# Sums of a Strassen-Winograd product on GpSimd, more W_in runs by seven products, and a new order

## The chip, the cores and the metric

The kernel runs on one core of a Trainium2 chip. A core has five engines with queues of their own: TensorE (PE, matmuls; its weight loads are shown as PEld), VectorE (DVE), ScalarE (ACT), GpSimd (POOL) and SyncE (SP, which here issues DMAs alone). Each engine takes its instructions in order; semaphores make one engine wait for another. The metric is the device time of one execution in microseconds (us), the median of several runs.

## The reference

Attention over a window of 96 positions and 8 global ones, with a bias that falls with the distance, then two matrices with a function between:

```python
# q, k, v: (4, 8, 768, 64); w_in: (512, 2048); w_out: (2048, 512); scale = 1/8
scores = scale * q @ k^T - slope[h] * dist      # kept where 0 <= i - j < 96 or j < 8
a = softmax(scores); attn = a @ v               # (4, 8, 768, 64)
x = attn.transpose(0, 2, 1, 3).reshape(3072, 512)
h = x @ w_in
g = h - tanh(h)
out = g @ w_out                                 # (3072, 512), float32
```

## The kernel before

The 3072 rows are 24 units of 128 rows. A unit's queries and keys come in by DMA (`lq`, `lk`, with values `lv`), are transposed (`T`, on TensorE for the first seven units and by a transposing DMA on SP for the rest), multiplied (`S`), put through the exponential (`E`, ScalarE), masked (`M`, VectorE, line 405, from the fourth unit on), multiplied with the values (`AV`), scaled by the inverse of the row sum (`R`, `N`) and transposed again (`X`, `Xe`). `K` and `V` are small copies of the global keys and values.

Units are then grouped for the first matrix: two groups of one unit, five of two, three of four (groups 7, 8 and 9). For a column block f of 128 of the 2048 columns, `m1` is a product of W_in with the group's transposed rows (line 470), `th` its tanh (ScalarE, line 567) and `g` the difference (VectorE, line 581), written as bfloat16 into `gall`. With four units a block is four matmuls of 128x512.

The table DUNITS names runs of four column blocks (group, run) that are computed in another way: as a 2x2 by 2x2 block product with seven instead of eight half-size products (the Strassen-Winograd scheme). `v1` to `v4` are its sums of W_in (VectorE, line 502), once for each run number, `y1` to `y4` its sums of the group's rows (line 507), `d1` to `d7` the seven products of four 128x256 matmuls each (line 529), `e0` to `e2` copies of partial results from PSUM (ScalarE, line 272), `q11`, `q21`, `q22` three adds (VectorE, lines 540 and 543). Tanh and difference then stand at lines 554 and 560. Before, runs 2 and 3 of groups 8 and 9 are done so.

The second matrix is done in the same scheme for each pair of units (a, a+1), twelve pairs: `w1` to `w4` are sums of W_out, computed once (line 608). `n1` to `n4` are sums of blocks of `gall` (`g_sum`, line 610; 128x1024 bfloat16 each, two of them in place): `n1` is read by `n2` and by product `p5`, `n2` by `n4` and `p6`, `n3` by `p7`, `n4` by `p3`. The products `p1` to `p7` are eight matmuls of 128x256 (line 636). `a0` to `a2` copy partial results, `c11` to `c22` add up the output blocks (line 650), `st` stores a unit's rows. For the last pair (22), `p3` and `c12` are split into two halves.

No scheduler orders this. The string ORDER lists each step's word, with a suffix for its engine where the step may go to more than one (`/a` ScalarE, `/d` VectorE, `/p` GpSimd, `/s` SyncE); the program issues the words in that order, and each engine's queue is the list filtered to it. The string HOMES gives the buffer or PSUM bank of each tile. GpSimd issues nearly all loads and some of the stores; an instruction that waits on GpSimd's queue holds back the loads behind it. A load there waits until the eighth load before it has landed.

Of the kernel before, what the change touches and what calls it, by code (L numbers as in the profile page):

```python
# [27 lines left out]
Xe.5/d th.0.12 g.2.14 m1.3.6 E.6.1 g.0.12 m1.3.8 n3.0 th.3.6 lk.10 E.6.0 n2.0 m1.3.4 g.3.6 K.6/a m1.3.2 n1.2 w1.0
m1.3.12 th.3.2 lk.8 g.0.8 th.3.8 p1.0 w1.1 m1.3.10 w3.0 a0.0/a th.3.12 g.3.2 m1.3.0 lv.6 th.3.10 w2.0 p2.0 w2.1 lq.10
w3.1 p6.0 T.7 lv.7 w4.1 p7.0 g.3.8 a1.0/a V.5/a n2.2 p5.0 th.3.0 T.9 n3.2 g.3.12 p1.2 a2.0/a w4.0 p2.2 a0.2/a g.3.10  # L30
th.3.4 p6.2 c11.0 T.8 c22.0 M.6.0 p4.0 a1.2/a n4.2 p5.2 g.3.0 g.3.4 p7.2 a2.2/a c21.0 c11.2 p3.2 st.1.0/p T.10 v1.3
M.6.1 lk.12 S.7 c12.2/a c22.2 lk.14 AV.6 n4.0 E.7.1 p4.2 V.6/d lk.11 R.6 E.7.0 N.6/d m1.3.14 lk.13 M.7.1 X.6 M.7.0
th.3.14 p3.0 lq.12 Xe.6/a c21.2 g.3.14 AV.7 lq.11 c12.0/a K.7/d R.7 S.8 N.7/d lv.8 n1.4 X.7 lv.9 E.8.1 p1.4 Xe.7/d n2.4
lv.10 m1.4.8 E.8.0 v1.2 v2.3 lq.13 m1.4.10 a0.4/a M.8.1 th.4.8 K.9/a p6.4 g.4.8 th.4.10 E.9.0 g.4.10 m1.4.14 a1.4/d S.9
V.7/d th.4.14 M.9.0 T.11 g.4.14 p5.4 E.9.1 M.8.0 T.12 m1.4.4 E.10.0 n3.4 p2.4 M.9.1 st.3.0/s th.4.4 M.10.0 E.10.1 AV.8
n4.4 m1.4.0 T.13 lq.15 K.10/a R.8 a2.4/a N.8/d AV.9 th.4.0 g.4.4 p3.4 Xe.8 R.9 N.9/d m1.4.2 c12.4/a c11.4 Xe.9 m1.4.6
g.4.0 st.4.0/p th.4.2 M.10.1 lq.14 m1.4.12 th.4.6 g.4.2 lv.11 p7.4 g.4.6 th.4.12 lk.15 S.10 c22.4 V.9/d lv.13 g.4.12
p4.4 E.11.0 n1.6 st.2.0/p p2.6 E.12.0 K.11/d lv.12 n3.6 AV.10 n2.6 K.12/a E.11.1 lk.16 p1.6 R.10 c21.4 lq.16 N.10/a
m1.5.10 a0.6/d M.11.1 p6.6 c11.6 th.5.10 S.11 T.15 a1.6/d g.5.10 p5.6 E.13.1 M.12.0 T.14 m1.5.8 V.10/d n4.6 E.13.0
M.11.0 m1.5.14 Xe.10 E.12.1 M.13.1 AV.11 th.5.14 p7.6 R.11 th.5.8 a2.6/d M.12.1 N.11/a m1.5.12 V.11/d v3.2 p3.6 g.5.14  # L40
th.5.12 M.13.0 Xe.11 m1.5.0 c12.6/a c22.6 st.6.0/p g.5.8 m1.5.2 th.5.0 lv.14 T.16 g.5.12 AV.12 g.5.0 th.5.2 lq.19 m1.5.6
R.12 N.12/d lk.18 m1.5.4 th.5.6 g.5.2 lq.18 p4.6 g.5.6 th.5.4 lq.17 g.5.4 S.12 V.12/d lv.16 c21.6 p1.8 n1.8 E.14.1 lv.15
m1.6.4 a0.8/d E.14.0 K.15/d v2.2 lk.17 AV.13 n2.8 th.6.4 m1.6.14 K.14/d lk.19 R.13 E.15.0 g.6.4 p6.8 N.13/d th.6.14 T.18
p2.8 g.6.14 a1.8/a M.14.0 Xe.12 S.13 n4.8 p5.8 c11.8 E.16.1 st.5.0/s v4.3 M.14.1 m1.6.10 E.16.0 M.15.0 T.17 AV.14 n3.8
E.15.1 m1.6.12 R.14 N.14/d T.19 th.6.10 m1.6.0 M.15.1 m1.6.2 a2.8/d th.6.0 Xe.14 M.16.0 V.14/a m1.6.6 g.6.0 th.6.2 Xe.13
g.6.10 AV.15 th.6.6 m1.6.8 g.6.2 g.6.6 p3.8 th.6.8 R.15 N.15/d th.6.12 p7.8 c12.8/a g.6.8 Xe.15 K.16/a st.8.0/p p1.10
g.6.12 lv.19 c22.8 S.14 n1.10 a0.10/a lq.21 n2.10 p4.8 E.17.1 lv.17 M.16.1 p6.10 E.17.0 V.15/d lk.20 p2.10 a1.10/d lk.23
v4.2 c21.8 p5.10 K.17/d lk.21 n4.10 st.9.0/s AV.16 M.17.1 a2.10/a lv.18 E.18.0 m1.7.15 R.16 N.16/d lq.22 p3.10 th.7.15
c11.10 lq.20 g.7.15 S.15 V.16/d c12.10/d lk.22 m1.7.6 M.17.0 E.19.0 lq.23 m1.7.7 E.19.1 M.19.0 lv.20 m1.7.5 M.18.0
th.7.6 T.21 th.7.7 m1.7.10 g.7.6 th.7.5 n3.10 m1.7.11 E.18.1 M.19.1 AV.17 th.7.10 g.7.5 m1.7.12 th.7.11 M.18.1 T.20  # L50
m1.7.2 R.17 g.7.7 th.7.12 N.17/d m1.7.9 Xe.16 th.7.2 g.7.12 AV.19 g.7.2 th.7.9 m1.7.0 T.22 V.17/d R.19 g.7.11 m1.7.4
th.7.0 g.7.9 st.7.0/s K.19/a m1.7.3 T.23 N.19/d th.7.4 v3.3 m1.7.8 g.7.10 Xe.17 g.7.0 p7.10 th.7.8 V.19/d th.7.3 g.7.8
m1.7.1 st.10.0/s Xe.19 g.7.4 m1.7.14 th.7.1 g.7.3 m1.7.13 c22.10 th.7.14 g.7.1 p4.10 g.7.14 th.7.13 g.7.13 S.16 c21.10
p1.12 n1.12 E.21.0 n2.12 p2.12 E.20.1 n3.12 AV.18 a0.12/d K.21/a E.20.0 p6.12 R.18 N.18/d K.20/a n4.12 S.17 Xe.18
a1.12/a c11.12 M.21.0 p5.12 E.22.1 M.20.1 p7.12 a2.12/d E.21.1 n1.14 p3.12 K.22/a M.20.0 E.22.0 S.18 c22.12 n2.14
c12.12/a p4.12 E.23.1 st.12.0/p n3.14 lv.23 m1.8.1 c21.12 E.23.0 y1.8 lv.21 d1.8.2 y2.8 p2.14 M.22.1 e0.8.2/a lv.22
M.21.1 th.8.1 d6.8.2 M.23.0 AV.20 p1.14 R.20 V.20/d M.22.0 d2.8.2 a0.14/a n4.14 m1.8.2 e1.8.2/a y3.8 N.20/a c11.14 p6.14
M.23.1 g.8.1 d7.8.2 th.8.2 d5.8.2 a1.14/d AV.21 q11.8.2 e2.8.2/a p5.14 R.21 V.21/a N.21/d d3.8.2 g.8.2 Xe.21 AV.22
th.8.9 q22.8.2 m1.8.0 th.8.8 R.22 y4.8 V.22/a Xe.20 m1.8.4 N.22/d g.8.9 d4.8.2 th.8.4 st.0.0/s d1.8.3 g.8.8 th.8.0 Xe.22
d2.8.3 q21.8.2 e0.8.3/a AV.23 g.8.4 th.8.11 d6.8.3 m1.8.5 R.23 q11.8.3 e1.8.3/a N.23/d d5.8.3 d7.8.3 g.8.0 Xe.23  # L60
e2.8.3/a m1.8.7 th.8.5 q22.8.3 th.8.10 d3.8.3 g.8.11 a2.14/a d4.8.3 th.8.7 g.8.5 m1.8.3 th.8.12 q21.8.3 p3.14 g.8.7
th.8.15 g.8.12 m1.8.6 th.8.13 g.8.15 d2.9.2 th.8.6 g.8.13 m1.9.2 c12.14/a y1.9 th.8.14 st.14.0/s g.8.6 m1.9.0 th.9.2
st.13.0/s y2.9 th.8.3 g.8.14 d1.9.3 d1.9.2 g.8.3 p7.14 e0.9.2/a g.8.10 e0.9.3/a m1.9.1 n1.16 th.9.0 y3.9 d6.9.2 c22.14
th.9.1 d6.9.3 g.9.2 p4.14 e1.9.3/a g.9.0 e1.9.2/a g.9.1 d5.9.3 d2.9.3 y4.9 e2.9.3/a d7.9.3 n2.16 d5.9.2 q22.9.3 p1.16
e2.9.2/a q11.9.2 d4.9.3 c21.14 a0.16/d d7.9.2 st.15.0/p m1.9.4 q22.9.2 st.11.0/p n3.16 d3.9.3 th.9.4 d3.9.2 q11.9.3
p6.16 th.9.9 q21.9.3 th.9.13 g.9.9 d4.9.2 a1.16/a m1.9.6 th.9.8 g.9.4 n1.18 p5.16 th.9.6 q21.9.2 th.9.12 m1.9.3 g.9.6
g.9.12 p1.18 th.9.14 g.9.13 a2.16/a th.9.15 p2.16 n3.18 a0.18/a th.9.3 p7.16 c11.16 n2.18 m1.9.7 c22.16 g.9.8 p2.18
g.9.15 th.9.11 p4.16 th.9.10 g.9.11 g.9.3 m1.9.5 n4.18 p6.18 n4.16 p7.18 g.9.14 a1.18/a th.9.5 g.9.10 p5.18 th.9.7 g.9.5
p3.16 a2.18/d c21.16 p2.20 g.9.7 st.17.0/s c12.16/a st.16.0/s n1.20 p1.20 n2.20 p3.18 a0.20/a c22.18 c11.18 p6.20 n3.20
c12.18/a st.18.0/s p4.18 a1.20/d n1.22 p5.20 n3.22 p7.20 n2.22 a2.20/a c21.18 p1.22 c22.20 st.19.0/s c11.20 p2.22  # L70
a0.22/a p6.22 c11.22 n4.22 st.22.0/s p4.20 a1.22/a p5.22 c21.20 n4.20 st.21.0/p p7.22 a2.22/a p3.20 c22.22 p4.22
# [758 lines left out]
```

## Time and profile before

| what | value |
|---|---|
| median of 3 runs | 202.23 us (202.12 to 202.49) |
| the profiled execution's own time | 202.65 us |
| its span, first to last instruction | 200.9 us |
| TensorE clock granted | 1.0 throughout |
| VectorE sums of `g_sum` | 48 of 128x1024, 684 ns each |
| GpSimd busy | 72.9 us, nearly all of it DMA issues of 0.6 to 0.9 us |

The profile is of one execution. Busy time of an engine is shown as a sum, a share of the span, or by groups of instructions of one source line; a group's row has its count, its busy time and the mean of one, then the idle time of the engine just before these instructions and what ended it. The chain of waits follows the work that ended last back to the start. A busy share of 97% says that an engine is a candidate, and the stretches of time say where.

### The profile page before, as it was taken

Reading aid. Unit: us, or ns where it says so; the run is one execution under the profiler, and the core shown is the slowest. Engines: PE = TensorE matmul, PEld = TensorE weight load, DVE = VectorE, ACT = ScalarE, POOL = GpSimd, SP = SyncE. Lnnn points to the kernel's source line nnn. Section 1 sums busy time; section 2 is a strip of 40 time slices with the busy share of each in tenths; the row PEclk is TensorE's granted clock in tenths of the full one; section 3 lists DMA queues with packets and bytes.
Section 4 is the critical chain, followed back from the end, with each engine's and each line's share of the span. In section 5 each row is a group of like instructions: output and inputs, shape, how many; then the busy total and the mean of one; then the engine's idle time right before and its main releaser. Section 6 shows DMA issues by size and latency. Waiting matters only on the chain.

```text
span 200.9 us, 5510 instructions
## 1 busy us (share of the span) xinstructions
PE 194.4 (97%) x2195; PEld 155.5 (77%) x2195; DVE 178.5 (89%) x375; ACT 132.6 (66%) x245; POOL 72.9 (36%) x93
## 2 busy tenths in 40 slices
...
GB/s 145 217 184 184 195 166 207 198 156 145 144 194 161 192 160 182 131 169 152 207 155 145 167 156 167 210 28 58 74 51 110 66 43 104 0 3 106 90 96 131
DMA packets 103755, 27.36 MB, mean 136 GB/s; under 512 B 93921, under 2 KB 101345, under 8 KB 103729
## 3 DMA queue, kind: packets, MB, share of 16 engines
...
q14 instruction: 10, 0.07, 0.1%
HBM read 27.26 MB, written 6.29 MB: 167 GB/s over the span
## 4 chain that ended last, share of the span: by engine, by line
PE 69%; DMA 13%; DVE 8%; POOL 7%; issue 1%; ACT 0%; POOLq 0%; DVEq 0%
PE ps L636 31%; PE ps L470 24%; DMA w_out_bf<-in_moe_w_out_dram 7%; DMA w_in_bf<-in_moe_w_in_dram 6%; PE ps L529 6%; PE ps L420 4%; PE ps L394 4%; DVE gall L581 2%; POOL w_in_bf L343 2%; POOL vb L340 2%; POOL mem L337 1%; DVE mem L405 1%; DVE wc L608 1%; DVE ot L650 1%; DVE gall L621 1%
## 5 line engine op out<-in xcount | busy, mean ns | idle before, releaser
L470 PE MATMUL ps<-xT,w_in_bf 128*128 128x256 bf16 (+2 forms) x576 | 77.2, 284 | 1.0 <-DMA w_in_bf<-in_moe_w_in_dram 0.9
L470 PEld LDWEIGHTS <-w_in_bf 128*128 128x128 bf16 x576 | 50.2, 98 | 15.9 <-DMA w_in_bf<-in_moe_w_in_dram 1.1
L567 ACT ACTIVATE th<-ps 128x512 f32<-128x512 f32 (+1 forms) x82 | 47.1, 594 | 16.8 <-PE ps L470 14.6
L581 DVE TENSOR_TENSOR gall<-ps,th 128x512 bf16<-128x512 f32 (+1 forms) x82 | 52.9, 667 | 5.9 <-ACT th L567 5.2
L636 PEld LDWEIGHTS <-gall 128*128 128x128 bf16 x488 | 46.3, 98 | 7.6 <-issue 0.5
L401 ACT ACTIVATE mem<-ps 128x1024 bf16<-128x1024 f32 x44 | 43.3, 1027 | 7.9 <-PE ps L394 7.0
L653 POOL DMA_DIRECT2D out_dram<-ot x10 | 5.7, 572 | 105.2 <-DVE ot L650 66.9
L636 PE MATMUL ps<-w_out_bf,gall 128*128 128x256 bf16 (+1 forms) x296 | 36.4, 270 | 0.4 <-ACT ot L272 0.4
L405 DVE TENSOR_TENSOR mem<-mem,mk 128x1024 bf16<-128x1024 bf16 x40 | 26.3, 680 | 0.0
L636 PE MATMUL ps<-f,ss 128*128 128x256 bf16 x192 | 24.9, 273 | 0.0
L636 PE MATMUL ps<-wc,gall 128*128 128x256 bf16 x192 | 24.9, 273 | 0.0
L272 ACT COPY sn<-ps 128x256 f32<-128x256 f32 x23 | 8.6, 372 | 20.8 <-PE ps L636 20.8
L340 POOL DMA_DIRECT2D vb<-in_v_dram x24 | 21.5, 907 | 1.8 <-ACT sn L272 1.6
L340 POOL DMA_DIRECT2D mem<-in_q_dram x20 | 18.0, 908 | 9.5 <-PE ps L420 5.4
L636 PEld LDWEIGHTS <-ss 128*128 128x128 bf16 x192 | 18.4, 98 | 3.2
L340 POOL DMA_DIRECT2D mem<-in_k_dram x20 | 18.1, 915 | 4.6 <-DMA w_out_bf<-in_moe_w_out_dram 3.7
L650 DVE TENSOR_TENSOR ot<-ps,sn 128x256 f32<-128x256 f32 x36 | 14.6, 416 | 4.1 <-PE ps L636 3.1
L420 PEld LDWEIGHTS <-mem 128*128 128x128 bf16 x352 | 13.4, 97 | 2.3 <-ACT mem L401 0.5
L437 DVE TENSOR_TENSOR x<-ps,rden 128x512 bf16<-128x512 f32 x21 | 14.4, 687 | 0.6
L420 PE MATMUL ps<-vb,mem 128*128 128x65 bf16 x352 | 14.7, 193 | 0.1
L394 PE MATMUL ps<-mem 64*128 64x128 bf16 x352 | 13.2, 217 | 0.3 <-DVE gall L581 0.3
L394 PEld LDWEIGHTS <-mem 64*128 64x128 bf16 x352 | 10.0, 94 | 3.4 <-issue 2.4
...
## 6 DMA issues: line engine op xcount, KB each, us to landing
...
w_out_bf<-in_moe_w_out_dram POOLq DMA_DIRECT2D x4, 512.0 KB, 10.7
...
w_in_bf<-in_moe_w_in_dram POOLq DMA_DIRECT2D x2, 512.0 KB, 11.5
```

Source lines behind the costliest of these rows:

```text
L340: eng(e).dma_start(out=dst, in_=rows_of(src, u).rearrange("h p d -> p h d"))
L394: nc.tensor.matmul(bank(("s", u, o), hh)[:, p * P : (p + 1) * P], buf(("qk", back[u] if o else u))[r, 1, p, :], buf(("qk", u))[r, 0, p, :] ...
L401: nc.scalar.activation(d, banks(("s", u, o), 0, 1), AF.Exp, bias=0.0, scale=scale)
L405: nc.vector.tensor_tensor(out=t, in0=t, in1=mk[:, mask_of(u, o)], op=ALU.mult)
L420: nc.tensor.matmul(t[:, h // (H // 2), h % (H // 2), :], buf(("p", u, o))[:, slot(h), :], buf(("v", back[u] if o else u))[:, h, 0 : Dh + 1 ...
L437: nc.vector.tensor_tensor(out=buf(("x", u)).rearrange("q (a h) d -> q a h d", a=2), in0=t[:, :, :, 0:Dh], in1=rden.to_broadcast([P, 2, H / ...
L470: nc.tensor.matmul(t[:, (f - f0) * n : (f - f0 + 1) * n], w_in_bf[j][:, c, fo : fo + P], x[:, c, 0:n], start=(c == 0), stop=(c == CD - 1),)
L529: nc.tensor.matmul(t[:, r * 2 * P : (r + 1) * 2 * P], w(r)[:, c], x[:, c], start=first and r + c == 0, stop=c == 1, skip_group_check=not f ...
L567: nc.scalar.activation(h_view(buf(("th", g, f0)), g, m), h_view(bank(("h", g, f0)), g, m), AF.Tanh, bias=0.0, scale=1.0)
L581: nc.vector.tensor_tensor(out=o, in0=v(h), in1=v(th), op=ALU.subtract)
L636: nc.tensor.matmul(bank((holder, a))[:, c0:c1], s(f), t(f)[:, c0:c1], start=first and f == 0, stop=f == HF - 1, skip_group_check=not first,)
L650: nc.vector.tensor_tensor(out=o, in0=bank((holder, a))[:, 0:DH2], in1=buf(("sn", a, k)), op=ALU.add)
```

## The change

Three things change. First, `g_sum` takes its engine from the order's suffix, and 17 of its 48 sums go to GpSimd: `n1.0`, `n2.0`, `n3.0`, `n4.2`, `n4.4`, `n3.10`, `n3.12`, `n2.14`, `n4.14`, `n3.14`, `n1.16`, `n1.18`, `n3.18`, `n2.18`, `n1.22`, `n3.22`, `n4.22` (the number behind the point is the pair). Second, DUNITS gains run 1 of groups 8 and 9: eight `m1` words of four 128x512 matmuls go, and for each group come seven `d` products, three `e` copies and three adds, with four sums `v1.1` to `v4.1` once. Third, ORDER and HOMES are new from about the 24th microsecond on, with some small copies on the other of ScalarE and VectorE, and some stores on the other queue.

```diff
-    DUNITS = [(8, 2), (8, 3), (9, 2), (9, 3)]
+    DUNITS = [(8, 1), (8, 2), (8, 3), (9, 1), (9, 2), (9, 3)]
...
-    def g_sum(a, k):
+    def g_sum(e, a, k):
...
-        nc.vector.tensor_tensor(out=o(), in0=x(), in1=y(), op=op)
+        eng(e).tensor_tensor(out=o(), in0=x(), in1=y(), op=op)
...
-            op((f"n{k}", a), DVE, lambda e, a=a, k=k: g_sum(a, k))
+            op((f"n{k}", a), None, lambda e, a=a, k=k: g_sum(e, a, k))
```

The end of the order string, before and after:

```diff
-c12.20/a st.20.0/s p3.22.0 c21.22 c12.22.0/a p3.22.1 st.23.0/s st.22.256/p c12.22.1/d st.22.384/s
+a2.22/d c22.22 p3.22.0 c12.20/a p4.22 st.20.0/s c12.22.0/d st.22.256/s p3.22.1 c21.22 c12.22.1/d st.23.0/s st.22.384/s
```

GpSimd's queue where the second matrix is loaded, before (`w_out_bf_76` to `_79` are the four parts `out.0` to `out.3`, `vb` values, `mem` queries and keys):

```order
L340 DMA vb_87<-in_v_dram 128x8x64
L346 DMA w_out_bf_77<-in_moe_w_out_dram 128x4x512
L346 DMA w_out_bf_76<-in_moe_w_out_dram 128x4x512
L346 DMA w_out_bf_78<-in_moe_w_out_dram 128x4x512
L346 DMA w_out_bf_79<-in_moe_w_out_dram 128x4x512
L340 DMA mem<-in_q_dram 128x8x64
L340 DMA mem<-in_k_dram 128x8x64
```

and now:

```order
L343 DMA vb_87<-in_v_dram 128x8x64
L349 DMA w_out_bf_76<-in_moe_w_out_dram 128x4x512
L349 DMA w_out_bf_77<-in_moe_w_out_dram 128x4x512
L624 TENSOR_TENSOR ss_106<-gall 128x1024
L349 DMA w_out_bf_78<-in_moe_w_out_dram 128x4x512
L349 DMA w_out_bf_79<-in_moe_w_out_dram 128x4x512
L624 TENSOR_TENSOR ss_107<-ss_106,gall 128x1024
L343 DMA mem<-in_k_dram 128x8x64
L624 TENSOR_TENSOR gall<-gall 128x8x128
```

Three sums (`n1.0`, `n2.0`, `n3.0`; new line numbers are three higher) stand among the loads; two parts of the second matrix and all later queries and keys are behind the first of them.

VectorE's queue where the sums of pairs 16 and 18 stand, before (`ss` and `gall` rows of L621 are the sums, `th` rows the differences, L543 and L540 the adds, L650 the output blocks):

```order
L621 TENSOR_TENSOR ss3_109<-gall_105 128x1024
L543 TENSOR_TENSOR mem_81<-ps_61,mem_81 128x512
L581 TENSOR_TENSOR gall_105<-ps_61,th3_104 128x2x256
L560 TENSOR_TENSOR gall_105<-ps_61,th2_103 128x2x256
L560 TENSOR_TENSOR gall_105<-ps_61,th1_102 128x2x256
L621 TENSOR_TENSOR gall_105<-gall_105 128x8x128
L650 TENSOR_TENSOR ot1_117<-ps_61,sn0_111 128x256
L621 TENSOR_TENSOR ss2_108<-ss3_109,gall_105 128x1024
```

and now:

```order
L653 TENSOR_TENSOR ot0_116<-ps_61,sn0_111 128x256
L624 TENSOR_TENSOR gall_105<-gall_105 128x8x128
L563 TENSOR_TENSOR gall_105<-ps_61,th2_103 128x2x256
L546 TENSOR_TENSOR mem_81<-ps_61,mem_81 128x512
L563 TENSOR_TENSOR gall_105<-ps_61,th1_102 128x2x256
L546 TENSOR_TENSOR mem_81<-ps_61,mem_81 128x512
L624 TENSOR_TENSOR gall_105<-gall_105,ss3_109 128x8x128
```

Of pair 18 the sums `n1`, `n3` and `n2` have left this queue for GpSimd's; `n3` and `n4` of pair 16 are still here, and the adds of the new runs stand between.

More of the change, by code (lines that the diff above doesn't have):

```diff
@@ L28 @@
[L28 to L71, printed above, removed]
-c12.20/a st.20.0/s p3.22.0 c21.22 c12.22.0/a p3.22.1 st.23.0/s st.22.256/p c12.22.1/d st.22.384/s
+m1.0.4 lv.5 th.1.4 g.1.4 T.4.1 m1.2.4 Te.4.1/a g.2.0 th.0.4 S.4 th.2.4 g.0.4 out.0 m1.1.8 E.4.0 g.2.4 m1.2.8 E.4.1 M.4.0
@@ new lines @@
+lk.9 n1.2/d p7.0 n2.2/d a1.0/a lq.10 th.3.6 w4.0 p5.0 lv.7 c11.0 g.3.12 p1.2 a2.0/a th.3.10 w4.1 T.8 p2.2 n3.2/d a0.2/a
+th.3.2 c22.0 p6.2 n4.0/d g.3.10 n4.2/p p4.0 a1.2/a g.3.6 p5.2 c11.2 g.3.2 T.9 p7.2 a2.2/a g.3.4 c21.0 p3.2 c22.2 T.10
+st.1.0/p M.6.0 S.7 lk.12 c12.2/a AV.6 E.7.0 lk.11 p4.2 R.6 K.7/d V.6/d N.6/d E.7.1 lv.9 m1.3.14 M.7.0 lq.11 X.6 M.7.1
+th.3.14 p3.0 Xe.6/a lq.12 g.3.14 AV.7 c12.0/a c21.2 lv.8 R.7 S.8 N.7/d st.2.0/p n1.4/d X.7 E.8.1 p1.4 lq.13 Xe.7/d
+n2.4/d m1.4.8 E.8.0 lk.13 a0.4/d K.9/d M.8.1 m1.4.10 lk.16 th.4.8 g.4.8 p6.4 lv.10 th.4.10 T.11 E.9.0 g.4.10 m1.4.14
@@ new lines @@
+st.3.0/s a1.4/a S.9 th.4.14 T.12 g.4.14 p5.4 E.9.1 M.9.0 m1.4.0 E.10.0 M.9.1 m1.4.4 T.13 V.7/d E.10.1 n3.4/d AV.9 M.8.0
+a2.4/a p2.4 th.4.4 R.9 N.9/d V.9/a m1.4.6 K.10/d M.10.1 Xe.9 AV.8 g.4.4 n4.4/p th.4.6 m1.4.2 c11.4 th.4.0 R.8 N.8/d
+m1.4.12 th.4.2 g.4.0 Xe.8 p7.4 lv.11 th.4.12 g.4.6 p3.4 lk.14 c22.4 g.4.2 p4.4 lv.12 c12.4/a g.4.12 M.10.0 S.10 lq.14
+c21.4 p1.6 n1.6/d lq.15 E.11.1 K.11/d K.12/d n2.6/d p2.6 lk.15 a0.6/a E.11.0 v1.2 AV.10 st.0.0/p c11.6 p6.6 E.12.0 lv.13
+R.10 N.10/d m1.5.10 a1.6/a lq.16 M.11.1 V.10/a M.11.0 S.11 th.5.10 v1.1 T.14 p5.6 g.5.10 E.13.1 M.12.0 m1.5.8 E.12.1
@@ new lines @@
+p7.8 E.15.1 n4.8/d AV.14 M.15.0 T.17 E.16.1 m1.6.0 R.14 v2.3 M.15.1 a2.8/a m1.6.6 T.18 c22.8 V.14/d m1.6.10 N.14/d
+th.6.6 Xe.13 th.6.0 g.6.6 AV.15 th.6.10 m1.6.12 v3.3 g.6.10 Xe.14 m1.6.8 R.15 th.6.12 g.6.0 p4.8 N.15/d th.6.8 g.6.12
+Xe.15 m1.6.2 c21.8 g.6.8 st.9.0/p p3.8 th.6.2 T.19 lq.21 g.6.2 p2.10 c12.8/a lk.22 n1.10/d p1.10 lv.19 n2.10/d S.14
+a0.10/a M.16.0 V.15/a lk.21 p6.10 M.16.1 E.17.0 lq.22 K.17/d a1.10/d E.17.1 AV.16 n4.10/d lv.17 p5.10 E.18.0 lq.20
+m1.7.4 a2.10/d lk.20 R.16 N.16/d m1.7.15 th.7.4 g.7.4 p3.10 th.7.15 c11.10 T.21 m1.7.2 g.7.15 c12.10/a st.10.0/p v4.3
@@ new lines @@
+n3.12/p N.18/d p6.12 K.20/a K.21/a c11.12 Xe.18 c21.10 S.17 a1.12/d V.19/d p5.12 n1.14/d lv.21 Xe.16 E.21.1 n4.12/d
+lv.22 p7.12 a2.12/a M.20.0 E.22.1 lv.23 p3.12 K.22/d c22.12 v4.1 E.22.0 M.21.1 p4.12 M.22.1 S.18 c21.12 AV.20 c12.12/d
+E.23.1 M.21.0 p1.14 st.12.0/s st.5.0/s M.22.0 E.23.0 m1.8.0 y1.8 y2.8 V.20/a d2.8.1 R.20 y4.8 th.8.0 d1.8.1 N.20/d
+n2.14/p a0.14/a AV.21 e0.8.1/a g.8.0 d1.8.3 d2.8.3 R.21 e0.8.3/a N.21/d d6.8.1 V.21/a p2.14 Xe.21 y3.8 e1.8.1/a M.23.0
+AV.22 c11.14 d6.8.3 Xe.20 R.22 d5.8.1 N.22/d d7.8.1 e2.8.1/a q11.8.1 d1.8.2 Xe.22 e1.8.3/a q22.8.1 d3.8.1 e0.8.2/a p6.14
@@ new lines @@
+M.23.1 th.8.4 V.22/d n4.14/p th.8.5 d5.8.3 g.8.4 d4.8.1 e2.8.3/a g.8.5 d6.8.2 a1.14/a q21.8.1 d2.8.2 e1.8.2/a AV.23
+q11.8.3 th.8.7 d5.8.2 R.23 d3.8.3 N.23/d e2.8.2/a d7.8.2 th.8.6 g.8.7 Xe.23 d7.8.3 th.8.13 q22.8.2 n3.14/p d3.8.2
+th.8.12 m1.8.3 q22.8.3 st.13.0/s q11.8.2 p5.14 g.8.12 d4.8.2 g.8.6 a2.14/a d4.8.3 th.8.9 q21.8.2 p3.14 th.8.8 q21.8.3
+m1.8.1 g.8.13 g.8.9 p7.14 th.8.1 y3.9 th.8.11 m1.8.2 y1.9 c12.14/a g.8.8 th.8.15 st.14.0/p m1.9.2 c22.14 th.8.3
+st.11.0/p g.8.11 d1.9.2 y2.9 th.8.10 p4.14 g.8.1 e0.9.2/a g.8.10 th.8.2 d2.9.1 g.8.3 d6.9.2 th.8.14 d1.9.1 c21.14
```

115 lines of the change are left out of this document (68 added, 47 removed).

## The prediction

> **What bounds the kernel now.** I read the page's shares first, then busy time in stretches, then the chain of waits, and last the groups of instructions. The share of each engine alone misleads here:
>
> ```profile
> PE 194.4 (97%) x2195; PEld 155.5 (77%) x2195; DVE 178.5 (89%) x375; ACT 132.6 (66%) x245; POOL 72.9 (36%) x93
> ```
>
> TensorE and VectorE both look full and GpSimd idle. The stretches tell which one sets the end (columns: stretch, its length, then busy time and count of PE, PEld, DVE, ACT and POOL, granted clock, DMA share, GB/s):
>
> ```profile
> 20.00:30.00 10.00, 9.93 (x152) 8.86 (x151) 7.40 (x14) 8.50 (x16) 6.06 (x8) 1.00 1.85 181
> 30.00:40.00 10.00, 9.88 (x146) 8.88 (x145) 9.18 (x17) 8.79 (x17) 4.81 (x6) 1.00 1.31 203
> ...
> 41.00:58.60 17.60, 17.20 (x210) 14.90 (x208) 17.51 (x35) 9.17 (x18) 8.78 (x11) 1.00 2.02 159
> 58.60:100.00 41.40, 41.40 (x542) 36.44 (x540) 39.16 (x84) 32.25 (x61) 19.91 (x24) 1.00 1.74 167
> 100.00:140.00 40.00, 39.99 (x432) 28.41 (x431) 38.78 (x78) 27.88 (x47) 13.13 (x16) 1.00 1.22 140
> 140.00:160.00 20.00, 20.00 (x197) 14.68 (x195) 19.57 (x39) 15.40 (x36) 1.16 (x2) 1.00 0.49 64
> 160.00:180.00 20.00, 20.00 (x161) 15.64 (x160) 19.68 (x37) 11.93 (x23) 1.13 (x2) 1.00 0.14 51
> ```
>
> From 58.6 to 180 us TensorE lacks 0.01 us of being busy all the time, while VectorE has 2.24, 1.22, 0.43 and 0.32 us free. TensorE is the bound there and VectorE follows close behind it. Only between 41 and 58.6 us is VectorE the fuller one (17.51 of 17.60 us), and TensorE loses 0.40 us. The chain of waits says the same (start, length, what):
>
> ```profile
> 27.59 13.26 DMA w_out_bf<-in_moe_w_out_dram
> 40.85 0.60 DVE wc L608
> ...
> 57.48 0.70 DVE x L437
> ...
> 58.62 0.87 PE ps L636 x8
> ...
> 179.73 17.05 PE ps L636 x160
> 197.13 0.62 PE ps L636 x8
> ```
>
> The last load of W_out lands at 40.85 us, VectorE carries the chain to 58.2 us, and TensorE carries it to the end. So time can be gained by fewer TensorE cycles, or by the few tenths that TensorE idles. VectorE time by itself is worth nothing after 58.6 us.
>
> **Part 1: seven products in place of sixteen matmuls.** For groups 8 and 9 the second run of four W_in columns was four `m1` words of four 128x512 matmuls. Now it is seven `d` words of four 128x256 matmuls. The chain has both kinds back to back:
>
> ```profile
> 153.64 0.86 PE ps L470 x4
> 154.51 0.87 PE ps L529 x8
> ```
>
> Sixteen cost 4 x 0.86 = 3.44 us, 28 cost 28/8 x 0.87 = 3.05 us: 0.39 us less for a group, **-0.8 us** for both, on the path, because TensorE has no other wait there. That holds only while VectorE and ScalarE deliver.
>
> What they get in return comes from these groups (busy us, mean ns | idle before):
>
> ```profile
> L621 DVE TENSOR_TENSOR ss<-gall 128x1024 bf16<-128x1024 bf16 x12 | 8.2, 684 | 0.1
> L272 ACT COPY mem<-ps 128x512 f32<-128x512 f32 x12 | 6.9, 589 | 2.9 <-PE ps L529 2.8
> L543 DVE TENSOR_TENSOR mem<-ps,mem 128x512 f32<-128x512 f32 x8 | 5.5, 685 | 0.3 <-ACT mem L272 0.2
> L540 DVE TENSOR_TENSOR ps<-ps,mem 128x512 f32<-128x512 f32 x4 | 2.7, 684 | 0.0
> L502 DVE TENSOR_TENSOR mem<-w_in_bf 128x512 bf16<-128x512 bf16 x4 | 1.6, 411 | 0.0
> L274 DVE COPY sn<-ps 128x256 f32<-128x256 f32 x13 | 5.4, 414 | 1.3 <-PE ps L636 1.3
> L278 POOL IOTA rel<- 128x256 bf16 x1 | 0.3, 343 | 0.4 <-POOLq L811 0.4
> ```
>
> VectorE gains six adds (`q11`, `q21`, `q22`) of 0.685 = 4.1 us and four sums of W_in at 0.41 = 1.6 us. ScalarE gains six copies of 0.589 = 3.5 us; it has 4.6 us free between 140 and 160 us alone, so they hide, and without that cover they would delay tanh by as much. VectorE loses seventeen sums of 0.684 = 11.6 us, eight of them between 125 and 180 us, where the six adds go: 5.5 out, 4.1 in. The small copies that change sides (`a`, `c12`, `K`, `V`, `N`) give back some 1.5 us over the whole span. VectorE ends 4 us lighter, so it stays behind TensorE. I cost all of this at nothing.
>
> **Part 2: what a GpSimd sum takes.** No row shows one. From below, the same sum takes 0.684 us on VectorE. GpSimd's only arithmetic is the iota row: 343 ns for 256 elements written, 1.37 us for 1024. A sum reads two operands and writes one: one pass 1.37, two passes 2.7, three in sequence 4.1 us. I take 2.1 us, between one pass and two, since that row is the nearest; 0.7 to 4.1 us are the ends. The Trainium skill's GPSIMD Engine Reference, section 3.1, has about 2.6 cycles for each element of a two-operand operation at 1.2 GHz, which is an estimated 2.2 us here and would leave the sum below as it is.
>
> Does it fit? The distance between a sum and the product that reads it is TensorE work in the new order. A product of eight matmuls is the 0.87 us row above. Five of the seventeen (`n4.2`, `n4.4`, `n3.12`, `n2.18`, `n3.22`) have three products between: 2.6 us. The rest have 3.5 us or more. At 2.1 us none is late.
>
> Early, GpSimd also issues the loads, and its sums now stand among them:
>
> ```profile
> 26.03 2.31 POOL L346 DMA_DIRECT2D w_out_bf<-in_moe_w_out_dram  x3 [1.92 <-DMA w_in_bf<-in_moe_w_in_dram]
> 28.63 2.10 DVE L581 TENSOR_TENSOR gall<-ps,th 128x512 bf16<-128x512 f32 x3
> ...
> w_out_bf<-in_moe_w_out_dram POOLq DMA_DIRECT2D x4, 512.0 KB, 10.7
> ```
>
> Sum `n1.0` waits for the last tanh difference of the second unit (the third of the row at 28.63, ending 30.7 us; moved some 2 us forward in the new order), and `out.2` and `out.3` are queued behind it: issued near 31 instead of 26.8 and 27.6 us. The last one took 13.26 us to land (the chain's row) against a median of 10.7 us, so the four stand in line. Its later issue is free as long as the line before it does not run empty: the load issued at 26.03 us lands at about 26.0 + 10.7 = 36.7 us, so an issue by 33 us costs nothing. If GpSimd took 4.1 us, `out.3` would come some 2 us late, and the VectorE work at 40.85 us with it.
>
> The three sums of the first pair and `n4.2` take 2.7 us from VectorE before 58 us, where TensorE lost 0.40 us to it. I count half, **-0.2 us**, since N, M and the sums of W_out still stand in a row on VectorE; the ends are 0 and -0.6 (with the 0.07 and 0.12 us of 20 to 40 us).
>
> **Part 3: the tail.** The last two half products stood one behind the other, and the second waited for the copy of the first:
>
> ```profile
> 197.13 0.61 PE L636 MATMUL ps<-w_out_bf,gall 128*128 128x128 bf16 x8 [0.35 <-ACT ot L272]
> ```
>
> The new order puts `p4.22` (0.87 us) between them, which covers the copy: **-0.35 us**. `c21.22` then ends beside the last half product, so the final add and stores keep their distance to it.
>
> **Sum.** -0.8 - 0.2 - 0.35 = -1.35 us. The profiled execution has a span of 200.9 us, which would become 199.55; its own run took 202.65 us, 1.75 us around the span. The median of the runs shown is 202.23 us, so the forecast is 202.23 - 1.35 = **200.9 us**.
>
> **The rivals.**
>
> *A: GpSimd's sums come late (slower).* Place: the five products with 2.6 us. Price: each is late by what a sum takes beyond 2.6 us, and TensorE has no idle time to regain it. It turns the gain of 1.35 us over from 5 x (t - 2.6) = 1.35, t = 2.87 us. At 3.2 us the time is 200.9 + 3.0 = 203.9 us, at 4.1 us 208.4. For it: three passes would be 4.1 us, and the loads share the engine. Against: the iota row would have to be exceeded more than twofold. Chance 0.20.
>
> *B: VectorE is held while GpSimd sums (no change).* The two engines would exclude each other where a VectorE instruction reads both operands from SBUF (masks, L405; sums, L621 and L507; copies K and V). Before, GpSimd had no arithmetic beside VectorE, so no row speaks for or against. In the new order such an instruction stands at least 2.2 us of TensorE work behind 15 of the 17 sums; at 2.1 us these are not held. `K.5` stands right behind `n2.0`, `V.19` 1.7 us behind `n3.12`: holds of 2.1 and 0.4 us. The first falls where VectorE has 0.8 us free (30 to 40 us), so 1.3 us reach TensorE: 200.9 + 1.3 = 202.2 us. Were instructions with a PSUM operand held too (L581, L543), 17 x 2.1 = 36 us of VectorE would be lost against about 8 us free (the 4.2 us of the stretches and the 4 us that it is lighter), some 229 us. Chance 0.13, and 0.03 for the wider hold.
> The Trainium skill, SBUF — State Buffer, section "SBUF: two separate sides", calls the port pair of VectorE and GpSimd "an **exclusive lock**, not a bandwidth split", for VectorE instructions with two SBUF inputs against a GpSimd one that reads SBUF. By that rule the narrow hold happens and the wide one does not; the trace before cannot show it.
>
> *C: the gains all come.* Every idle tenth after 20 us goes: -0.8 - 0.35 - 0.6 = -1.75, 200.5 us. This lies within the forecast's side.
>
> **How the numbers follow.** Forecast and C together 0.64, A 0.20, B 0.13, the wide hold 0.03. A measurement of this kernel tells 0.2% from no change, 0.4 us, so faster is below 201.8 us: 0.64. Within: B, 0.13. Slower: 0.23. The range runs from C with the scatter of the runs (202.12 to 202.49), 200.2 us, to rival A near 3.15 us for a sum, 203.7 us; what is beyond is the rest of A and the wide hold, under 2 in 10. The forecast's own range is 200.2 to 201.8 us.
>
> **What would show it.** Right: TensorE again busy throughout from 60 to 195 us, about 0.8 us less of matmul work in the last two groups; the GpSimd rows of the sums at 1.4 to 2.6 us; no products waiting for GpSimd; `out.3` landing near 41 us; no idle time before the last half product. Wrong: L636's successor waiting for POOL at the five places (A); VectorE rows of two SBUF operands that are longer or start late beside a sum, or TensorE idle near 33 us (B); W_out landing after 42 us; six more copies making ScalarE the one that tanh waits for between 140 and 170 us.

## The result: slower by a tenth, and the profile after

The changed kernel takes 221.98 us (median of four runs, 221.39 to 223.42); the kernel before, beside it on the same chip, 202.36 us (202.12 to 202.79). The ratio is 1.098, with an interval of 1.092 to 1.104. The forecast was 200.9 us, its range ended at 203.7 us. The profiled execution has a span of 219.8 us, 18.9 us more than before. Some executions of the experiments' kernels were longer, most of them at a lower clock, and are left out of the ratios; in experiments 4, 5, 6 and 12 the time given is therefore the ratio times the time of the kernel before, and from the profiles of 4, 5 and 6 only lengths of instructions are read.

The shares of the page (busy time, share of the span, instructions) show one odd thing: VectorE's busy time rose from 178.5 to 191.8 us, though it has fewer instructions to do.

```profile
PE 197.5 (90%) x2212; PEld 158.8 (72%) x2219; DVE 191.8 (87%) x371; ACT 133.4 (61%) x234; POOL 112.7 (51%) x111
```

Next the stretches, with the columns of the prediction's view (stretch, length, busy PE, PEld, DVE, ACT, POOL, clock, DMA share, GB/s):

```profile
20.00:41.00 21.00, 17.62 (x269) 15.53 (x266) 17.12 (x28) 14.81 (x25) 14.35 (x13) 1.00 1.56 187
41.00:58.60 17.60, 17.60 (x186) 15.49 (x184) 16.63 (x34) 8.65 (x18) 12.30 (x13) 1.00 1.66 150
58.60:100.00 41.40, 39.62 (x542) 34.70 (x540) 38.90 (x78) 29.48 (x49) 24.75 (x29) 1.00 1.73 159
100.00:140.00 40.00, 37.85 (x407) 26.77 (x406) 37.03 (x72) 27.73 (x51) 18.41 (x18) 1.00 1.28 140
140.00:160.00 20.00, 17.53 (x201) 14.54 (x197) 18.63 (x32) 12.70 (x21) 9.24 (x7) 0.91 0.83 81
160.00:180.00 20.00, 17.83 (x156) 14.18 (x157) 19.96 (x35) 14.52 (x29) 5.72 (x5) 1.00 0.18 60
180.00:200.00 20.00, 18.14 (x151) 14.59 (x151) 19.86 (x29) 9.63 (x20) 6.50 (x3) 1.00 0.01 2
```

TensorE, which lacked nothing from 58.6 to 180 us before, now lacks 1.78, 2.15, 2.47, 2.17 and 1.86 us in the stretches from 58.6 to 200 us, and 3.38 us between 20 and 41 us; from 41 to 58.6 us it is fuller than before (17.60 against 17.20). The loss is spread over the span, and from 160 to 200 us VectorE has next to no free time left (0.04 and 0.14 us). So the question is what VectorE does there. Its groups, by form:

```profile
L408 DVE TENSOR_TENSOR mem<-mem,mk 128x1024 bf16<-128x1024 bf16 x40 | 32.6, 835 | 0.2
L624 DVE TENSOR_TENSOR ss<-ss,gall 128x1024 bf16<-128x1024 bf16 x9 | 9.9, 1097 | 0.1
L546 DVE TENSOR_TENSOR mem<-ps,mem 128x512 f32<-128x512 f32 x12 | 8.0, 678 | 0.0
L624 DVE TENSOR_TENSOR ss<-gall 128x1024 bf16<-128x1024 bf16 x8 | 7.3, 915 | 0.0
```

Before, the sums had a mean of 684 ns, and the masks of 680:

```profile
L405 DVE TENSOR_TENSOR mem<-mem,mk 128x1024 bf16<-128x1024 bf16 x40 | 26.3, 680 | 0.0
```

Now the means are 835, 1097 and 915 ns, while the adds that read a PSUM operand (L546) stay at 678. A mean that rises while the work is the same hides a few very long instructions. The view of one line shows them by minimum, median and maximum:

```profile
L624 DVE TENSOR_TENSOR ss<-ss,gall x9: 673/685/2600, 46.9 to 207.9; 128x1024 bf16<-128x1024 bf16 x9
L624 DVE TENSOR_TENSOR ss<-gall x8: 669/682/2560, 46.1 to 197.9; 128x1024 bf16<-128x1024 bf16 x8
L624 POOL TENSOR_TENSOR gall<-gall x6: 2128/2164/3714, 36.6 to 200.0; 128x1024 bf16<-128x1024 bf16 x6
L624 POOL TENSOR_TENSOR ss<-gall x4: 2109/2124/2127, 28.1 to 197.8; 128x1024 bf16<-128x1024 bf16 x4
```

A GpSimd sum takes 2.12 to 2.16 us, and some on either engine take much longer. The timeline tells where. VectorE between 119 and 125 us (start, length, line, operation, tiles):

```profile
119.90 3.31 DVE L408 TENSOR_TENSOR mem<-mem,mk 128x1024 bf16<-128x1024 bf16 x1
123.13 0.41 DVE L505 TENSOR_TENSOR mem<-mem,w_in_bf 128x512 bf16<-128x512 bf16 x1
```

and GpSimd in the same microseconds:

```profile
119.91 0.58 POOL L656 DMA_DIRECT2D out_dram<-ot  x1
120.50 2.15 POOL L624 TENSOR_TENSOR gall<-gall 128x1024 bf16<-128x1024 bf16 x1
122.58 0.93 POOL L343 DMA_DIRECT2D vb<-in_v_dram  x1
```

The mask `M.17.1` starts at 119.90 us and should end at 120.6. The sum `n3.10` starts at 120.50 and ends at 122.65, and the mask ends 0.56 us after that. It is not a wait for data: the mask's row has begun. I call this a hold. Nine VectorE rows are held so, each beside another GpSimd sum: `V.4` (2.85 us more than the median of its kind), `M.10.1` 1.93, `M.17.1` 2.62, `K.22` 2.72, `M.23.1` 1.60, `y4.9` 1.89, `n2.16` 1.91, `n1.20` 1.87, `n2.20` 1.79: 19.2 us together. The other direction exists too: `n3.12` took 3.71 us, `n4.2` 2.67 and `n2.18` 2.57. `n3.12` began at 136.54 us, while VectorE did two masks and a sum in a row until 138.26 us, and ended 1.99 us after them; a sum by itself takes 2.12.

That holds set the end is read from the chain of waits. It goes through VectorE at all nine: at six as a piece of 1.30 to 2.88 us that it calls issue (from 31.77, 70.17, 120.25, 142.96, 177.61 and 181.02 us), at `M.23.1` as 2.19 us of a mask, and near 200 us so:

```profile
198.00 2.49 DVE ss L624
200.49 0.02 issue
200.51 2.50 DVE ss L624
203.01 0.05 issue
203.06 6.97 PE ps L639 x47
```

Two sums of 0.68 us stand there with 2.5 us each. TensorE has nothing to do meanwhile, and the clock answers:

```profile
200.00:203.58 3.58, 0.78 (x8) 0.48 (x6) 3.54 (x4) 0.00 (x0) 2.44 (x1) 1.00 0.00 0
203.58:206.99 3.41, 3.41 (x18) 2.46 (x17) 1.38 (x3) 0.37 (x1) 0.00 (x0) 0.50 0.43 153
```

After a stretch with 0.78 us of work in 3.58 us, the granted clock is 0.50 for 3.41 us, up to 1.7 us lost. It happens once more at 145.56 us, behind the hold of `K.22`.

The account against the profiled execution before: TensorE idle from 20 to 200 us 13.8 us against 0.6 before (20 to 180 us, ahead of the tail), 2.8 us idle near 201 us, two windows at half clock 3.4 us: 19.4 us, where the span grew by 18.9.

### The profile page after: what moved, and what is told of

It is laid out like the page before. It is cut to its first block, busy times and chain, and to the rows that moved or that the text cites. A ratio compares the mean times of both kernels' runs of the same rounds, so it can differ in the third digit from the quotient of the medians.

```text
span 219.8 us, 5571 instructions
## 1 busy us (share of the span) xinstructions
PE 197.5 (90%) x2212; PEld 158.8 (72%) x2219; DVE 191.8 (87%) x371; ACT 133.4 (61%) x234; POOL 112.7 (51%) x111
## 4 chain that ended last, share of the span: by engine, by line
PE 57%; DVE 17%; issue 9%; DMA 8%; ACT 4%; POOL 4%; DVEq 0%; POOLq 0%; ACTq 0%
PE ps L639 28%; PE ps L473 18%; DMA vb<-in_v_dram 5%; PE ps L423 4%; PE ps L397 4%; DMA w_in_bf<-in_moe_w_in_dram 4%; DVE mem L408 3%; DVE ss L624 3%; DVE gall L563 3%; PE ps L532 3%; DVE gall L584 2%; DVE mem L546 2%; POOL vb L343 2%; POOL mem L340 1%; DVE ps L543 1%
## 5 line engine op out<-in xcount | busy, mean ns | idle before, releaser
L473 PE MATMUL ps<-xT,w_in_bf 128*128 128x256 bf16 (+2 forms) x538 | 69.0, 278 | 2.9 <-DVE ot L653 1.5
L473 PEld LDWEIGHTS <-w_in_bf 128*128 128x128 bf16 x544 | 46.9, 98 | 16.0 <-issue 2.6
L584 DVE TENSOR_TENSOR gall<-ps,th 128x512 bf16<-128x512 f32 (+1 forms) x74 | 47.8, 667 | 9.6 <-ACT th L570 9.0
L570 ACT ACTIVATE th<-ps 128x512 f32<-128x512 f32 (+1 forms) x74 | 42.3, 593 | 21.2 <-PE ps L473 15.7
L639 PEld LDWEIGHTS <-gall 128*128 128x128 bf16 x488 | 47.3, 99 | 9.7 <-issue 2.5
L408 DVE TENSOR_TENSOR mem<-mem,mk 128x1024 bf16<-128x1024 bf16 x40 | 32.6, 835 | 0.2
L275 ACT COPY sn<-ps 128x256 f32<-128x256 f32 x29 | 10.8, 373 | 22.4 <-PE ps L639 22.2
L624 POOL TENSOR_TENSOR gall<-gall,ss 128x1024 bf16<-128x1024 bf16 x4 | 9.1, 2266 | 26.7 <-PE ps L639 26.7
L624 POOL TENSOR_TENSOR gall<-gall 128x1024 bf16<-128x1024 bf16 x6 | 14.8, 2460 | 10.9 <-DVE ss L624 10.7
L423 PEld LDWEIGHTS <-mem 128*128 128x128 bf16 x352 | 13.8, 99 | 7.9 <-DVE mem L408 4.4
L624 POOL TENSOR_TENSOR ss<-gall 128x1024 bf16<-128x1024 bf16 x4 | 8.5, 2121 | 19.3 <-DVE gall L563 17.7
```

The source lines that it names most:

```text
L275: nc.scalar.copy(out=out, in_=in_)
L408: nc.vector.tensor_tensor(out=t, in0=t, in1=mk[:, mask_of(u, o)], op=ALU.mult)
L423: nc.tensor.matmul(t[:, h // (H // 2), h % (H // 2), :], buf(("p", u, o))[:, slot(h), :], buf(("v", back[u] if o else u))[:, h, 0 : Dh + 1 ...
L473: nc.tensor.matmul(t[:, (f - f0) * n : (f - f0 + 1) * n], w_in_bf[j][:, c, fo : fo + P], x[:, c, 0:n], start=(c == 0), stop=(c == CD - 1),)
L570: nc.scalar.activation(h_view(buf(("th", g, f0)), g, m), h_view(bank(("h", g, f0)), g, m), AF.Tanh, bias=0.0, scale=1.0)
L584: nc.vector.tensor_tensor(out=o, in0=v(h), in1=v(th), op=ALU.subtract)
```

## The experiments

Times are medians, with the ratio to the kernel before on the same chip (its medians were 202.07 to 202.39 us) and the ratio's interval. Theory H is the hold.

**1. All seventeen sums back on VectorE, the rest as changed.**

```diff
-n1.0/p ... n2.0/p ... n4.22/p
+n1.0/d ... n2.0/d ... n4.22/d
```

> The changed kernel with its seventeen sums on VectorE again; seven-product runs and order as changed. Theory H (VectorE is held while GpSimd sums): the ten long VectorE rows go, VectorE's busy time is 191.8 - 19.3 + 11.6 = 184 us, and the time is 200.5 to 204 us. Theory W (the new runs and the new order cost the time by themselves): 212 us or more, with TensorE waiting at the same places. Theory L (products wait for late GpSimd sums): also near 202 us, but then the changed kernel's trace should have had products released by GpSimd, and it has none.

208.01 us, ratio 1.030 (1.027 to 1.033). The masks are normal again:

```profile
L409 DVE TENSOR_TENSOR mem<-mem,mk 128x1024 bf16<-128x1024 bf16 x40 | 26.5, 682 | 0.1
```

14 us of the loss go with GpSimd's sums, though VectorE has 11.6 us more of them to do. So the hold is the larger part. But the time is above what H expected: some 6 us remain that no hold explains.

**2 and 3. Only the five early sums on GpSimd, and only the twelve late ones** (`n3.10` and later), the others on VectorE.

```diff
-n3.10/p ... n4.22/p      (2: late ones)
+n3.10/d ... n4.22/d
-n1.0/p n2.0/p n3.0/p n4.2/p n4.4/p      (3: early ones)
+n1.0/d n2.0/d n3.0/d n4.2/d n4.4/d
```

> The changed kernel with only the first five sums (n1.0, n2.0, n3.0, n4.2, n4.4) on GpSimd, the other twelve on VectorE. H: two holds stay, the copy V.4 (2.85 us over its normal time) and the mask M.10.1 (1.94 us); the time is 2 to 5 us above the kernel with all sums on VectorE. W and L: within 1 us of it.

> The changed kernel with only the last twelve sums on GpSimd, the first five on VectorE. H: up to eight holds of 1.6 to 2.7 us stay, 14.5 us in all, and the time is 8 to 17 us above the kernel with all sums on VectorE. W: no more than 2 us above it. L: 2 to 5 us above it, with products released by GpSimd.

213.24 us (1.055, 1.049 to 1.060) and 218.70 us (1.086, 1.077 to 1.095): 5.2 and 10.7 us above experiment 1 (the first just over the 5 us that H gave as its most), whose sum, 15.9 us, is more than the 14.0 us of all seventeen. In 2, `V.4` and `M.10.1` are held (4.9 us), in 3 the seven late rows (14.4 us), the same ones as in the changed kernel. The loss follows the held rows, not one place.

**4. The order of before with the same seventeen sums on GpSimd.**

```diff
-n1.0 ... n3.0 ... n4.22
+n1.0/p ... n3.0/p ... n4.22/p
```

> The kernel before, in its own order and with its own runs, only with the same seventeen sums on GpSimd. H: VectorE rows that read two SBUF operands are held up to 2.1 us each beside a sum; the time is 8 to 25 us above before, 210 to 227 us. W: within 2 us of before, since nothing but the engine of the sums differs. L: 4 to 8 us above, from the sums that stand 0.9 to 1.7 us ahead of their product, released by GpSimd and with VectorE rows of normal length.

The ratio is 1.076 (1.070 to 1.082), 1.076 x 202.07 = 217.4 us. Its masks:

```profile
L407 DVE TENSOR_TENSOR mem<-mem,mk 128x1024 bf16<-128x1024 bf16 x40 | 40.0, 1022 | 0.0
```

Here mostly other rows are held (`M.5.0` by 5.4 us, beside two sums, `y2.8` 4.1, `M.5.1` 2.6, `n3.16` 2.5). The hold does not belong to the new order: an order made without regard to it meets it as well.

**5. Only the nine sums beside which a row was held go back to VectorE**, the eight others stay on GpSimd.

```diff
-n2.0/p n4.4/p n3.10/p n2.14/p n3.14/p n1.18/p n3.18/p n1.22/p n3.22/p
+n2.0/d n4.4/d n3.10/d n2.14/d n3.14/d n1.18/d n3.18/d n1.22/d n3.22/d
```

> The changed kernel with the nine sums beside which a VectorE row was held (n2.0, n4.4, n3.10, n2.14, n3.14, n1.18, n3.18, n1.22, n3.22) back on VectorE; the other eight stay on GpSimd. H, if the neighbours stay as they were: no long VectorE rows, VectorE 8 x 0.68 = 5.5 us lighter than with all sums there, the time 1 to 4 us below that kernel's 208.0, so 204 to 207 us. H, if the eight meet other neighbours because everything before them now runs earlier: new holds of about 2 us each, 208 to 214 us. L (a GpSimd sum of 2.1 us is too late for its product): no better than 208 us, with normal VectorE rows.

Ratio 1.016 (1.011 to 1.020), 1.0158 x 202.16 = 205.4 us, 16.6 us below the changed kernel. The holds of all rows come to 0.5 us. Its masks:

```profile
L409 DVE TENSOR_TENSOR mem<-mem,mk 128x1024 bf16<-128x1024 bf16 x40 | 26.5, 683 | 1.2 <-ACT mem L405 1.1
```

Nine instructions of 0.68 us went onto an engine that is nearly full, and the time fell by 16.6 us. Of the theories tried, the hold alone explains that. The eight other sums are of use on GpSimd: 2.6 us less than experiment 1.

**6. The copies `V.4` and `K.22` on ScalarE.**

```diff
-V.4/d ... K.22/d
+V.4/a ... K.22/a
```

> The changed kernel with the two small copies that were held longest (V.4 2.85 us over its normal time, K.22 2.73 us) on ScalarE in place of VectorE. If such copies are held as the sums and masks are: both holds go and the time falls by 3 to 6 us, to 216 to 219 us. If their length was only the trace's way to show another wait: 221 to 223 us, with the same 2 us missing on the next VectorE row.

Ratio 1.092 (1.087 to 1.098), 1.0922 x 202.16 = 220.8 us: nothing to tell from the changed kernel's 1.098. Both copies' holds are gone, and the next instruction of the kind takes the hold in their place: `M.5.1` 2.69 us, `v4.1` 2.07 us. VectorE there:

```profile
32.69 0.69 DVE L409 TENSOR_TENSOR mem<-mem,mk 128x1024 bf16<-128x1024 bf16 x1 [0.33 <-ACT mem L405]
33.60 3.38 DVE L409 TENSOR_TENSOR mem<-mem,mk 128x1024 bf16<-128x1024 bf16 x1 [0.22 <-ACT mem L405]
```

beside GpSimd:

```profile
32.75 1.52 POOL L350 DMA_DIRECT2D w_out_bf<-in_moe_w_out_dram  x2
34.28 2.14 POOL L625 TENSOR_TENSOR ss<-ss,gall 128x1024 bf16<-128x1024 bf16 x1
```

The first mask runs beside a DMA issue at its normal 0.69 us; the second, which would have ended at 34.29 us, is held until the sum is over. The rows say that two-operand instructions are held by the sum, not by the issues.

**7. The disputed operation by itself.** Everything of the kernel is left out but a few tiles; VectorE does six instructions of one form beside three GpSimd sums, then the same beside three memsets of GpSimd.

```diff
+for form in FORMS:            # VectorE: 6 x form
+    3 x nc.gpsimd.tensor_tensor(mem, mem, mem)   # 128x1024 bf16; later: memset
```

> Everything is left out but a test of the two engines side by side: for each of six kinds of VectorE instruction, six of them run beside three GpSimd sums of 128x1024 bfloat16, and again beside three GpSimd memsets of the same tile. Kinds: add of two SBUF operands (bfloat16, then float32), add of a PSUM and an SBUF operand, bfloat16 copy within SBUF, float32 copy from PSUM, bfloat16 times a constant within SBUF. Narrow hold: beside the sums the two-SBUF adds have rows of 2 us or more over normal, the PSUM ones none. Wide hold: all kinds are held. If the reading of GpSimd is what holds, nothing is held beside the memsets; if any GpSimd arithmetic does, the same kinds are held there.

The timeline, beside sums first, then beside memsets (the length is that of the six together):

```profile
9.97 7.85 DVE L798 TENSOR_TENSOR mem<-mem 128x1024 bf16<-128x1024 bf16 x6
...
17.93 9.70 DVE L798 TENSOR_TENSOR ot<-th,th 128x512 f32<-128x512 f32 x6
...
27.69 4.31 DVE L798 TENSOR_TENSOR ot<-ps,th 128x512 f32<-128x512 f32 x6
27.92 6.52 POOL L818 TENSOR_TENSOR mem<-mem 128x1024 bf16<-128x1024 bf16 x3 [2.29 <-DVE mem L822]
...
34.75 8.11 DVE L804 COPY mem<-mem 128x1024 bf16<-128x1024 bf16 x6
...
42.97 4.31 DVE L805 COPY ot<-ps 128x512 f32<-128x512 f32 x6
...
50.03 8.11 DVE L806 TENSOR_SCALAR mem<-mem 128x1024 bf16<-128x1024 bf16 x6
...
58.38 4.32 DVE L798 TENSOR_TENSOR mem<-mem 128x1024 bf16<-128x1024 bf16 x6
...
63.02 4.32 DVE L798 TENSOR_TENSOR ot<-th,th 128x512 f32<-128x512 f32 x6
...
72.17 4.84 DVE L804 COPY mem<-mem 128x1024 bf16<-128x1024 bf16 x6
```

Two operands from SBUF cost 7.85 and 9.70 us beside sums and 4.32 beside memsets, in bfloat16 and in float32: two rows of the six and three of the six have 2.48 us each, the others 0.63 to 0.69. One operand from PSUM: 4.31, nothing. Copies and products with a constant inside SBUF: 8.11 us beside sums, so one operand suffices where the output lies in SBUF too. The 4.84 us beside memsets are not their normal length either. The six copies there by minimum, median and maximum, then a memset and the copy beside it:

```profile
L804 DVE COPY mem<-mem x6: 420/780/1134, 72.2 to 76.6; 128x1024 bf16<-128x1024 bf16 x6
72.38 1.10 POOL L825 MEMSET mem<- 128x1024 bf16 x1 [1.60 <-DVE mem L830]
72.62 1.13 DVE L804 COPY mem<-mem 128x1024 bf16<-128x1024 bf16 x1
```

Three copies took 1.13 us, each beside a memset, the three others 0.42. So the expectation's two cases both come true, each for its own forms: two-operand adds are held by a sum, which reads SBUF, and not by a memset, which reads nothing; copies and products with a constant are held by both. This is the list of forms to look for.

**8. The tail alone:** the kernel before, with `p4.22` between the two half products.

```diff
-p4.22 c12.20/a st.20.0/s p3.22.0 c21.22 c12.22.0/a p3.22.1
+c12.20/a st.20.0/s p3.22.0 p4.22 c21.22 c12.22.0/a p3.22.1
```

> The kernel before with one word moved: product p4.22 stands between the two halves of p3.22 instead of ahead of them. By the prediction's third part the 0.35 us that TensorE waited there for the copy go: 0.2 to 0.5 us below before. Against it: c21.22 now ends beside the last half product and its store of 256 KB is issued later, so the end could stay where it was, within 0.1 us of before.

201.97 us beside 202.16, ratio 1.0005 (0.998 to 1.003). The idle time before the last half product is gone in its profile, 0.0 in place of 0.35 us:

```profile
L637 PE MATMUL ps<-w_out_bf,gall 128*128 128x128 bf16 x16 | 1.2, 219 | 0.0
```

The wait went as forecast; whether 0.35 us were gained is below what the runs can tell.

**9 and 10. The changed order without the two new runs**, all sums on VectorE (9), or eight on GpSimd as in experiment 5 (10). Runs (8,1) and (9,1) are plain products again; several of their eight tiles lie in PSUM banks that other tiles still use, so parts of the output are others and waits for banks come in.

```diff
-d1.8.1 d2.8.1 d6.8.1 d5.8.1 d7.8.1 d3.8.1 d4.8.1 e0.8.1/a ... q11.8.1 ...
+m1.8.4 m1.8.5 m1.8.6 m1.8.7 ...
```

> The changed kernel's order with all sums on VectorE and without the new seven-product runs: the eight plain products, tanh and differences of run 1 of groups 8 and 9 stand where the seven products stood. VectorE loses six adds and four sums of W_in, 5.7 us, TensorE gains 0.8 us of work. If VectorE's load is what keeps the kernel with all sums on VectorE at 208.0 us: 202 to 205 us. If the new order is at fault: still 206 to 209 us.

> The same without the new runs, and with the eight sums on GpSimd beside which no VectorE row was held in the changed kernel (n1.0, n3.0, n4.2, n3.12, n4.14, n1.16, n2.18, n4.22). H, if no new neighbours meet: no long VectorE rows, VectorE 5.5 us lighter, and since TensorE is the bound then, 0 to 2 us below the kernel without runs and with all sums on VectorE. If neighbours meet anew: 2 us more for each hold that the trace shows.

209.94 us (1.036, 1.027 to 1.044) and 207.32 us (1.024, 1.017 to 1.031). Inconclusive on the runs, because of the added waits. That the eight sums on GpSimd gain (2.6 us here) is seen again, though in 10 one mask (`M.23.1`) met a sum anew and was held by 0.75 us.

**11 and 12. The same with a free bank for each tile**, the products of six of the tiles, and the tanh and differences of four, moved to where a bank is free.

```diff
-h.8.4:2 h.8.5:3 h.8.6:2 h.8.7:3 h.9.4:6 h.9.5:7 h.9.6:4 h.9.7:6
+h.8.4:2 h.8.5:3 h.8.6:2 h.8.7:3 h.9.4:6 h.9.5:7 h.9.6:2 h.9.7:3
-... th.8.4 ... g.8.4 ... m1.9.6 ...
+m1.8.4 ... th.8.4 g.8.4 ... g.9.12 m1.9.6 ...
```

> The changed order with all 17 sums on VectorE and runs (8,1) and (9,1) as plain products again, each of their eight column blocks in a PSUM bank that no other tile uses at that time. Theory R (the new runs' six adds and four sums, 5.7 us of VectorE work, fill VectorE between 140 and 190 us, and that makes most of the 6 us by which all-sums-on-VectorE stood over the kernel before): 202.5 to 205 us, VectorE below 19.8 of 20 us between 160 and 180 us. Rival O (the order itself loses it, whatever the runs): 206.5 to 210 us, with TensorE idle in the same places before 140 us.

> The same, with the eight sums that held nobody on GpSimd (n1.0, n3.0, n3.12, n4.14, n1.16, n2.18, n4.22 and the like; the nine others on VectorE). R: VectorE is then lighter than in the kernel before and TensorE sets the end: 201.5 to 203.5 us, so these sums on GpSimd gain up to 1.5 us over the kernel beside it, or nothing if TensorE already sets the end there. O: 204.5 to 208 us.

208.62 us (1.032, 1.029 to 1.036), and a ratio of 1.022 (1.016 to 1.027), 1.0217 x 202.39 = 206.8 us (with one mask, `M.23.0`, held by 1.58 us). O's numbers, not R's: experiment 11 stands beside experiment 1 (1.030), with or without the new runs. The stretch from 160 to 180 us, of experiment 1:

```profile
160.00:180.00 20.00, 18.90 (x158) 15.11 (x156) 20.00 (x38) 14.69 (x30) 1.14 (x2) 1.00 0.11 41
```

and of experiment 11, whose VectorE has the new runs' ten instructions less to do:

```profile
140.00:160.00 20.00, 19.08 (x191) 14.23 (x190) 17.95 (x36) 12.02 (x23) 0.00 (x0) 1.00 0.37 77
160.00:180.00 20.00, 18.10 (x142) 13.62 (x140) 20.00 (x38) 13.61 (x29) 1.14 (x2) 1.00 0.11 41
```

VectorE has 2 us free between 140 and 160 us and none between 160 and 180, where TensorE waits for it. Before, the same two stretches had 19.57 and 19.68: the order of before spreads VectorE's work more evenly. So the 6 us that are not holds belong to the new order, with its buffers and banks and the small copies and stores that it moves to other queues. Which of its many moves costs them was not separated.

No version was faster than the kernel before by more than the runs can tell.

## Why the prediction was wrong

**What bounds the kernel.** The reading was right: TensorE sets the end, VectorE follows close behind. What I made of it was too bold. VectorE's 4.2 us of free time in the four stretches from 58.6 to 180 us were its whole reserve there, and what takes more from it reaches TensorE. The holds took 19.2 us over the span.

**The step that failed** is in rival B: "In the new order such an instruction stands at least 2.2 us of TensorE work behind 15 of the 17 sums; at 2.1 us these are not held." Two things are wrong in it. It looked behind each sum only. All nine held instructions stand *ahead* of the sum in the order, by 4 steps (`M.10.1`) to 30 (`M.23.1`). The order fixes each engine's own sequence, but not how the two queues stand to each other in time: VectorE runs late against GpSimd, and so they meet. And a distance in TensorE work is no time: one hold moves all that follows on VectorE. The two instructions that the prediction named, `K.5` and `V.19`, were not held at all. It also counted the copies among the instructions that read two operands; they read one, and two of them were held all the same. The mechanism had 0.13 and a price of 202.2 us, where 40 masks and 31 sums on VectorE that any of 17 GpSimd sums could meet meant a price anywhere between 0 and 17 x 2.1 = 36 us: the range's end of 203.7 us did not cover it.

The Trainium skill, SBUF — State Buffer, section "SBUF: two separate sides", gives the rule that the prediction quoted: VectorE with two SBUF inputs and a GpSimd instruction that reads SBUF exclude each other. The trace agrees for the seven held rows with two operands and for the probe (7.85 against 4.32 us), and with the rule's limits (4.31 us with a PSUM operand, 4.32 beside memsets); the copies `V.4` and `K.22` have one input and are outside the rule as the prediction quoted it. The rule was known; its price was worked out from distances in the order, and these did not hold in time.

**A second step** failed beside it: the new order was taken as neutral apart from the edits counted. It costs 6 us without any GpSimd sum and without the new runs (experiment 11).

**The terms.** Part 1, -0.8 us for the new runs: experiments 1 and 11 differ by the two new runs, 1.030 against 1.032 with intervals that overlap, so a gain of that size is neither shown nor excluded. "VectorE ends 4 us lighter" was wrong as time: it ended 13.3 us busier (191.8 against 178.5), since a held instruction counts as busy. Part 2, the sum of 2.1 us: right, 2.12 to 2.16. No product waited for GpSimd and none of the five tight ones was late because of its length; rival A is false. No engine waited for a load that stands behind a sum in GpSimd's queue either. `out.2` and `out.3` were issued at 30.23 and 31.0 us, as worked out. They landed within 9.9 us, by 40.9 us at the latest. Between 41 and 58.6 us TensorE gained 0.40 us, where I counted 0.2; but it had lost 3.38 us between 20 and 41 us, so the stretch holds other work, and the term is not measured by it. Part 3: the idle time went, the gain could not be measured.

**The wide hold** is false: rows with a PSUM operand keep their lengths (678 ns, L546). **Rival C** failed with the forecast.
